# Seven block products for every two-sign unit, in one step of a five-step pipeline

## The chip, the cores and the metric

The kernel runs on one core of a Trainium2 chip. It uses TensorE (PE, matrix products), VectorE (DVE), ScalarE (ACT), GpSimd (POOL) and the DMA queues, of which SyncE (SP) and GpSimd issue the transfers. The metric is the time of one execution on the device in microseconds; before the change it is 1177.75 us, the median of three runs (1176.4 to 1179.02).

## The reference

The input x has 8 batches of 3136 tokens with 256 features. A two-dimensional Fourier transform over tokens and features is taken and its real part kept; each of the 25088 tokens then goes through a layer with 1024 hidden features:

```python
X = np.fft.fft(np.fft.fft(x, axis=1), axis=2).real
h = X.reshape(25088, 256) @ w_in                  # 256 -> 1024
e = np.exp(h - h.max(-1)); sm = e / (e.sum(-1) + 1e-09)
solu = h * sm
ln = (solu - solu.mean(-1)) / np.sqrt(solu.var(-1) + 1e-06) * g_ln
out = ln @ w_out                                  # 1024 -> 256
```

All of it is computed in fp32.

## The kernel before, in words

The transform over 3136 tokens is split as 49 x 64. The batches go in four pairs (`Pair`). For a pair, chunks of x are loaded twice, straight (`xa`, SP queue) and mirrored (`xb`, an indirect load on GpSimd's queue). `add_mirror` sums the two (GpSimd, L137 and L138; VectorE for the first pair), `fold` sums and subtracts mirrored features (VectorE, L128 and L129), `transform1` does the length-49 transform on TensorE (L182) and `keep` writes it to DRAM, from where `turn` reads it back in another order. There are 8 chunks of two parts each.

A *unit* is one frequency k1 of one pair: 128 tokens with the sign + and, except where k1 is 0, 128 more with the sign -. There are 25 units a pair, 100 in all; 96 have two signs and 4 (0, 25, 50, 75) have one. One pass of the main loop is a *step*; in step i the newest unit is i. For a unit:

- `transform2` (TensorE, L210) and the ScalarE copy `take2` (L216) give q; `spread` moves one row of it to a column r by a small DMA.
- `up` (TensorE, L238, 8 instructions of 512 columns) gives the even and the odd half of h in two PSUM tiles; `even` (VectorE, L244) and `join` for each sign (VectorE, L252) make h and its maximum.
- `expo` (ScalarE, L259 and L261) negates the maximum and takes u = exp(h - max) with its sum; `product` (VectorE, L268) makes u = h * u with its sum; `square` (ScalarE, L275) sums squares.
- `turn_blocks` (VectorE, L304) transposes blocks of 32 x 32 and `move_blocks` (16 DMAs on the SP queue for two units, L330) puts the blocks in their places, so that uT holds u transposed.
- `stats` (ScalarE) and `power` (GpSimd, L291) give the factor rs of each token.
- The *down* product u @ w_out is done lag = 4 steps later. `down` does it plainly: 8 blocks of 128 x 256 for a sign (L443). For odd two-sign units (`by_seven`) the two signs are done together: with u of both signs as a 2 x 2 matrix of blocks A11, A12 (sign +) and A21, A22 (sign -), a scheme of seven block products p1 to p7 (L359, each 4 blocks of 128 x 128) takes the place of eight. It needs four sums of blocks, S0 to S3, which GpSimd makes in `sums` (L354); p5 reads S0, p6 S1, p3 S3 and p7 S2. Weight sums Ws are made once. ScalarE's `keep` (L390) and VectorE's `finish` (L394) put the output together, `store` writes it: the + sign by SP, the - sign by an indirect DMA of GpSimd (L454).

The whole program is a hand schedule: each engine takes its instructions in the order in which the code emits them, and waits on semaphores for its inputs and for the buffers that it overwrites. In step i the seven products of an odd unit are spread over two steps: p1, p4, p2 in one, p5, p6, p3, p7 in the next, whose unit is done plainly beside them. `sums` and `power` come at the beginning of a step, and a step's order is, in short, `even`, `up`, `join`, first products, `expo`, other products, `product`, `square`, `turn_blocks`, `move_blocks`. Work for the next pair of batches (`ahead`) comes at the end: the mirror sum of a chunk in step f, its fold in f + 1, both parts of its first transform in f + 3, with f = 3, 5, ... 17 for pair 1, 27 to 41 for pair 2 and 51 to 65 for pair 3. S is one buffer (pool of one), uT, v, h and u are doubled.

Of the kernel before, what the change touches and what calls it, by code (L numbers as in the profile page):

```python
# [35 lines left out]
def kernel(  # L36
# [57 lines left out]

    def result(i):

        return ps_m.tile([P, 2 * D], FP32, tag=f"m{i % 4}", name="ps_m")
# [28 lines left out]
    def fold_features(o, i, copy):  # L126
        up, down = i[:, :, 1:128], i[:, :, 255:128:-1]
        nc.vector.tensor_tensor(out=o[:, :, 1:128], in0=up, in1=down, op=ALU.add)  # L128
        nc.vector.tensor_tensor(out=o[:, :, 129:256], in0=up, in1=down, op=ALU.subtract)  # L129
        copy(o[:, :, 0:129:128], i[:, :, 0:129:128])  # L130

    def add_mirror(pr, c, engine):

        xa, xb, _ = pr.raw[c]
        n = CH - 1 if c == NC - 1 else CH
        a, rb = xa[:, 0:n, :], xb[:, ::-1, :][:, 0:n, :]
        engine.tensor_tensor(out=a[:, :, 1:D], in0=a[:, :, 1:D], in1=rb[:, :, D - 1 : 0 : -1], op=ALU.add)  # L137
        engine.tensor_tensor(out=a[:, :, 0:1], in0=a[:, :, 0:1], in1=rb[:, :, 0:1], op=ALU.add)  # L138

    def fold(pr, c):  # L140

        xa, _, x0 = pr.raw.pop(c)
        y = xpool.tile([PR, CH, D], FP32, tag="y", name="y")
        copy = nc.scalar.copy if pr.p else nc.vector.tensor_copy
        fold_features(y, xa, copy)
        pr.y[c] = y
        if c == NC - 1:
            pr.y0 = xpool.tile([PR, 1, D], FP32, tag="y0", name="y0", bufs=1)
            fold_features(pr.y0, x0, copy)

    def transform1(pr, s):
# [6 lines left out]
        if l == 0:  # L158
# [3 lines left out]
            elif c < 4:  # L162
                z = fpool.tile([P, FF], FP32, tag="u", name="z_u", bufs=2)
                pr.z = z[0:ZR].rearrange("p (l d) -> p l d", l=CH)
# [82 lines left out]
    def join(t, s):  # L247

        if s == 0:
# [3 lines left out]
                                       scalar=-3.0e38, op0=ALU.add, op1=ALU.max, accum_out=t.nmax[:, s : s + 1])  # L253

    def expo(t, s):
        if s == 0:
            t.esum = small.tile([P, 2], FP32, tag="esum", name="esum")
            t.neg = small.tile([P, 2], FP32, tag="neg", name="neg")
        nc.scalar.mul(out=t.neg[:, s : s + 1], in_=t.nmax[:, s : s + 1], mul=-1.0)  # L259
        t.u[s] = fpool.tile([P, FF], FP32, tag="u", name="u", bufs=2)  # L260
        nc.scalar.activation(out=t.u[s], in_=t.h[s], func=ACT.Exp, bias=t.neg[:, s : s + 1],  # L261
                             accum_out=t.esum[:, s : s + 1])

    def product(t, s):
# [3 lines left out]
        nc.vector.scalar_tensor_tensor(out=t.u[s], in0=t.h[s], scalar=1.0, in1=t.u[s], op0=ALU.mult,  # L268
# [24 lines left out]
    class Batch:  # L293


        def __init__(self, by_blocks):
            if by_blocks:
                self.v = fpool.tile([P, 2, FF, 2], FP32, tag="v", name="v32", bufs=2)
            self.uT = fpool.tile([P, 2, KF, 4, 64], FP32, tag="uT", name="uT", bufs=2)

    def turn_blocks(t, s):

        for o in (s,) if len(t.signs) == 2 else (0, 1):
            nc.vector.transpose(out=t.batch.v[:, t.w, :, o], in_=t.u[s])  # L304
# [43 lines left out]
    def sums(t):  # L348

        A11, A12, A21, A22 = blocks(t)  # L350
        t.S = spool.tile([P, 4, KF // 2, P], FP32, tag="S", name="S")
        for j, (a, b, op) in enumerate(((A21, A22, ALU.add), (t.S[:, 0], A11, ALU.subtract),
                                        (A11, A21, ALU.subtract), (A12, t.S[:, 1], ALU.subtract))):
            nc.gpsimd.tensor_tensor(out=t.S[:, j], in0=a, in1=b, op=op)  # L354
# [5 lines left out]

    banks = []

    def bank(i):

        if not banks:
            banks.extend(result(j) for j in (2, 3, 1))
        return banks[i]

    class Down:
# [4 lines left out]

        def __init__(self, t, fresh):
            self.t = t
            self.C11, self.X, self.P53 = (bank(i)[:, 0:P] for i in range(3))
            self.A11, self.A12, _, self.A22 = blocks(t)
            for s in range(2):
                t.ot[s] = fpool.tile([P, D], FP32, tag="ot", name="ot", bufs=10)  # L380
# [3 lines left out]

        def place(self, s, half):
            return self.t.ot[s][:, half * P : (half + 1) * P]

        def keep(self, s, half, ps):

            nc.scalar.mul(out=self.place(s, half), in_=ps, mul=self.t.rs[:, s : s + 1])  # L390

        def add(self, s, half, ps):
            o = self.place(s, half)
            nc.vector.scalar_tensor_tensor(out=o, in0=ps, scalar=self.t.rs[:, s : s + 1], in1=o, op0=ALU.mult, op1=ALU.add)  # L394
# [7 lines left out]
        def p4(self):  # L402
            product7(self.P53, self.A22, Ws[:, 3], True)

        def keep4(self):
            self.keep(1, 0, self.P53)
# [4 lines left out]
        def keep11(self):  # L411
            self.keep(0, 0, self.C11)

        def p5(self):
            product7(self.P53, self.t.S[:, 0], Ws[:, 0], True)

        def keep5(self):
            self.keep(1, 1, self.P53)

        def p6(self):  # L420
            product7(self.X, self.t.S[:, 1], Ws[:, 1])

        def keep6(self):
            self.keep(0, 1, self.X)

        def p3(self):
            product7(self.P53, self.t.S[:, 3], Wo[:, KF // 2 :, P:])

        def p7(self):
            product7(self.X, self.t.S[:, 2], Ws[:, 2])  # L430

        def finish(self):
            self.add(0, 1, self.P53)
            self.add(1, 1, self.X)
            self.add(1, 0, self.X)
# [529 lines left out]
```

## Time and profile before

| what | value |
|---|---|
| median of 3 runs | 1177.75 us (1176.4 to 1179.02) |
| span of the profiled execution, which the page gives as its time | 1174.4 us |
| TensorE busy | 1132.6 us, 96% |
| VectorE busy | 1005.7 us, 86% |
| ScalarE busy | 762.4 us, 65% |
| GpSimd busy | 598.2 us, 51% |
| DMA, hardware queue and software queue | 60.4% and 12.4% of 16 engines |
| mean granted TensorE clock | 0.998 |
| first `up` of unit 5 and of unit 99 | 97.1 and 1127.0 us |

The page comes from one execution. A busy share is the part of the span in which an engine had an instruction running; matmuls overlap their neighbours, so a group's mean time is longer than the pitch at which they follow each other. The column "idle before" of a group says how long the engine had stood idle ahead of the group's instructions and who ended most of that. The timeline lists instructions of one kind in a row as one entry.

### The profile page before, as it was taken

The numbers are of one execution on the slowest core, as the hardware profiler recorded it, in microseconds if no ns is written. First come the engines' busy times: TensorE is split into PE (matmuls) and PEld (weight loads), VectorE is DVE, ScalarE is ACT, GpSimd is POOL, SyncE is SP. The second block draws the span as 40 slices with busy tenths as digits, with TensorE's granted clock in tenths as the row PEclk, the third lists the DMA queues.
The fourth block names the chain that finished last, engine by engine and source line by source line (L and its number), as shares of the span: only waits on it lengthen the run. The fifth ranks groups of instructions, "written<-read, shape, count | busy, mean of one in ns | idle before, by whom it ended". The sixth has DMA issues, their size and how long they took to land. (4 is left out here: it accounts for less than half of the span.)

```text
span 1174.4 us, 18577 instructions
## 1 busy us (share of the span) xinstructions
PE 1132.6 (96%) x5850; PEld 881.2 (75%) x5850; DVE 1005.7 (86%) x1376; ACT 762.4 (65%) x1841; POOL 598.2 (51%) x558
## 2 busy tenths in 40 slices
PE   2988999999999999999999999999999999999997
PEld 1556787777877787877877777778777787778787
DVE  7789999998878999998879999999887898888870
ACT  4577666757756766767656666676666676677651
POOL 3036666563465566563556666554544334433444
PEclk9999999999999999999999999999999999999999
DMA  9672998865988998865879898865775565745553
GB/s 243 196 186 71 180 183 180 176 141 127 180 185 167 182 167 186 176 141 135 176 146 188 176 188 183 172 146 133 153 154 135 135 152 125 154 108 137 130 116 109
DMA packets 458465, 185.55 MB, mean 158 GB/s; under 512 B 425750, under 2 KB 440350, under 8 KB 458368
## 3 DMA queue, kind: packets, MB, share of 16 engines
q1 hardware_dynamic: 444608, 146.22, 60.4%
q0 software_dynamic: 13760, 38.16, 12.4%
q8 instruction: 47, 0.77, 0.3%
q14 instruction: 50, 0.41, 0.1%
HBM read 44.78 MB, written 38.80 MB: 71 GB/s over the span
## 5 line engine op out<-in xcount | busy, mean ns | idle before, releaser
L443 PE MATMUL ps_m<-Wo,uT 128*128 128x256 f32 x1632 | 369.2, 380 | 3.1 <-ACT uT L321 2.1
L238 PE MATMUL ps_h<-Wi,q 128*128 128x512 f32 x800 | 360.8, 593 | 3.0 <-DVE nmax L252 2.1
L443 PEld LDWEIGHTS ps_m<-Wo,uT 128*128 128x128 f32 x1632 | 314.2, 196 | 33.8 <-ACT uT L321 2.4
L268 DVE SCALAR_TENSOR_TENSOR u<-h,u 128x1024 f32<-128x1024 f32 x196 | 266.1, 1366 | 50.5 <-ACT u L261 36.1
L238 PEld LDWEIGHTS ps_h<-Wi,q 128*128 128x128 f32 x800 | 145.9, 190 | 149.9 <-issue 140.0
L275 ACT ACTIVATE h<-u,usum 128x1024 f32<-128x1024 f32 x196 | 224.4, 1145 | 34.3 <-DVE u L268 33.0
L354 POOL TENSOR_TENSOR S<-uT 128x512 f32<-128x512 f32 x94 | 130.4, 1387 | 208.5 <-issue 138.7
L261 ACT ACTIVATE u<-h,neg 128x1024 f32<-128x1024 f32 x196 | 225.3, 1150 | 6.4
L304 DVE STREAM_TRANSPOSE v<-u 128x1024 f32<-128x1024 f32 x192 | 227.8, 1226 | 0.1
L291 POOL TENSOR_TENSOR rs<-v,neg_half 128x2 f32<-128x2 f32 (+1 forms) x100 | 71.7, 717 | 251.8 <-ACT v L284 251.7
L252 DVE CUSTOM_DVE_ANT_0 h<-ev,ps_h 128x1024 f32<-128x1024 f32 x100 | 122.2, 1222 | 33.3 <-PE ps_h L238 23.5
L244 DVE SCALAR_TENSOR_TENSOR ev<-w_mid,r,ps_h 128x1024 f32<-128x1024 f32 x100 | 126.7, 1267 | 25.6 <-PE ps_h L238 20.6
L359 PE MATMUL ps_m<-Ws,S 128*128 128x128 f32 x1128 | 141.5, 275 | 1.8 <-ACT ot L390 1.8
L216 ACT COPY q<-ps_m 128x256 f32<-128x256 f32 x100 | 36.8, 368 | 159.4 <-PE ps_m L210 155.9
L359 PEld LDWEIGHTS ps_m<-Ws,S 128*128 128x128 f32 x1128 | 133.6, 192 | 2.7 <-issue 1.6
L252 DVE CUSTOM_DVE_ANT_0 h<-h,ps_h 128x1024 f32<-128x1024 f32 x96 | 117.3, 1221 | 13.8
L454 POOL DMA_INDIRECT out_dram<-ot,idx x96 | 100.8, 1050 | 30.7 <-issue 18.7
L359 PE MATMUL ps_m<-Wo,uT 128*128 128x128 f32 x752 | 104.2, 282 | 0.1
L182 PE MATMUL ps_m<-y,F 98*100 98x258 f32 (+3 forms) x288 | 73.4, 390 | 24.7 <-DVE y L130 21.8
L210 PEld LDWEIGHTS ps_m<-T,g 128*128 128x128 f32 x400 | 60.2, 191 | 49.1 <-issue 41.7
L359 PEld LDWEIGHTS ps_m<-Wo,uT 128*128 128x128 f32 x752 | 96.1, 196 | 0.9 <-issue 0.5
L259 ACT ACTIVATE neg<-nmax 128x1 f32<-128x1 f32 x196 | 38.4, 196 | 81.5 <-DVE nmax L252 73.6
(87 smaller groups left out, 1186.7 us busy)
## 6 DMA issues: line engine op xcount, KB each, us to landing
uT<-v SPq DMA_DIRECT2D x752, 128.0 KB
out_dram<-ot SPq DMA_DIRECT2D x100, 128.0 KB
g<-zd POOLq DMA_DIRECT2D x72, 160.0 KB, 5.6
xa<-in_x_dram SPq DMA_DIRECT2D x28, 392.0 KB
zd<-z SPq DMA_DIRECT2D x24, 400.0 KB
raw_in<-in_moe_w_in_dram SPq DMA_DIRECT2D x4, 512.0 KB
raw_out<-in_moe_w_out_dram SPq DMA_DIRECT2D x2, 1024.0 KB
r<-q SPq DMA_DIRECT2D x100, 0.5 KB
```

The costliest lines, as they stand in the source:

```text
L182: nc.tensor.matmul(o[..., cs], F[:, 2 * t + h, :], i[..., cs], start=first, stop=True, skip_group_check=True)
L238: nc.tensor.matmul(ps[:, fs], t.q[:, c * P : (c + 1) * P], Wi[:, c, fs], start=True, stop=True)
L244: nc.vector.scalar_tensor_tensor(out=t.ev, in0=w_mid, scalar=t.r, in1=ps, op0=ALU.mult, op1=ALU.add)
L252: nc.vector.tensor_tensor_reduce(out=t.h[s], in0=t.h[0] if s else t.ev, in1=t.odd, scale=1.0 if s else -0.5, scalar=-3.0e38, op0=ALU.add, ...
L261: nc.scalar.activation(out=t.u[s], in_=t.h[s], func=ACT.Exp, bias=t.neg[:, s : s + 1], accum_out=t.esum[:, s : s + 1])
L268: nc.vector.scalar_tensor_tensor(out=t.u[s], in0=t.h[s], scalar=1.0, in1=t.u[s], op0=ALU.mult, op1=ALU.mult, accum_out=t.usum[:, s : s + 1])
L275: nc.scalar.activation(out=t.h[s], in_=t.u[s], func=ACT.Square, bias=t.usum[:, s : s + 1], scale=-float(FF), accum_out=t.ssq[:, s : s + 1])
L304: nc.vector.transpose(out=t.batch.v[:, t.w, :, o], in_=t.u[s])
L354: nc.gpsimd.tensor_tensor(out=t.S[:, j], in0=a, in1=b, op=op)
L359: nc.tensor.matmul(o, a[:, c], b[:, c], start=start and c == 0, stop=c == n - 1, skip_group_check=True)
L443: nc.tensor.matmul(ps, uT[:, c, :, s], Wo[:, c, :], start=(c == 0), stop=(c == KF - 1))
L454: dma = nc.gpsimd.indirect_dma_start(out=out, out_offset=bass.IndirectOffsetOnAxis(ap=idx[:, i : i + 1], axis=0), in_=t.ot[s], in_offset=None)
```

## The change

What the new code does, part by part:

- `by_seven` holds for every two-sign unit but the last (95 units, where it was 47). All seven products are done in one step, five steps behind the unit (lag 5), in the order p1, p4, p5, first-transform part, p2, p6, p3, p7. Plain products are left for the one-sign units and the last unit.
- C11 and X share one PSUM tile of two banks, p4's and p5's results share a bank. ScalarE evicts each pair in one instruction (`keep_p`, `keep_cx`); `finish` has two VectorE instructions, of 128 and 256 columns. `keep_cx` stands ahead of the step's `expo` on ScalarE, `finish` between the two `product`s on VectorE.
- S is four tiles, still one of each. `sums` for the next unit is emitted after p7, and its first sum gets a wait on the last `product` of the unit before (`behind`). So does each mirror sum.
- The mirror sum, the fold and the first transform of a chunk are cut in halves, one to a step: mirror in f and f + 1, fold in f + 1 and f + 2 (now between `join` and `product`), transform in f + 3 and f + 4. The sum of feature 0 goes from GpSimd to VectorE (one small instruction a half). The loads of x are emitted a step later.
- `move_blocks` is emitted in the next even step, after `sums`, where it was emitted at the end of the odd step.
- u is one tile for both signs, and one transpose instruction turns both (`turn_both`).
- h is kept negated (the weights' scale changes its sign), so `join` takes a minimum, the exponential uses scale -1 and the negation of the maximum is gone.

```diff
-    def sums(t):
+    S = [spool.tile([P, KF // 2, P], FP32, tag=f"S{j}", name=f"S{j}") for j in range(4)]
+
+    def sums(t, prv):
         A11, A12, A21, A22 = blocks(t)
...
+        for j, a, b, op in ((0, A21, A22, ALU.add), (1, S[0], A11, ALU.subtract), (3, A12, S[1], ALU.subtract),
+                            (2, A11, A21, ALU.subtract)):
+            i = nc.gpsimd.tensor_tensor(out=S[j], in0=a, in1=b, op=op)
+            if j == 0 and prv:
+                behind(i, prv)
...
+            self.CX = pair_cx[:, :, 0:P]
+            self.C11, self.X = (self.CX[:, i] for i in range(2))
+            self.PP = result(1)[:, 0 : 2 * P]
+            self.P4, self.P5 = (self.PP[:, i * P : (i + 1) * P] for i in range(2))
...
         def finish(self):
-            self.add(0, 1, self.P53)
-            self.add(1, 1, self.X)
-            self.add(1, 0, self.X)
+            o = self.t.ot[0][:, P:]
+            nc.vector.scalar_tensor_tensor(out=o, in0=self.P5, scalar=self.t.rs[:, 0:1], in1=o, op0=ALU.mult, op1=ALU.add)
+            o = self.t.ot[1].rearrange("p (i d) -> p i d", i=2)
+            nc.vector.scalar_tensor_tensor(out=o, in0=self.X.unsqueeze(1).to_broadcast([P, 2, P]),
+                                           scalar=self.t.rs[:, 1:2], in1=o, op0=ALU.mult, op1=ALU.add)
...
+            if work == "mirror" and a in (0, 1):
+                behind(add_mirror(pr, c, nc.gpsimd, a), units[i - 1])
+            if work == "fold" and a in (1, 2):
+                fold_part(pr, c, a - 1)
+
+    def behind(i, t):
+
+        tc.add_manual_dep(i.ins, t.last.ins.name,
+                          mybir.DependencyInfo(mybir.DependencyClass.Sync, mybir.DependencyReason.DATA),
+                          reason="two operands at a time from SBUF")
...
-        lag = 4
+        lag = 5
...
-            return i % 2 and i < len(units) - 1 and len(units[i].signs) == 2
+            return 0 <= i < len(units) - 1 and len(units[i].signs) == 2
...
                 enter(i)
                 even(cur, up(cur, 0))
                 cur.odd = up(cur, 1)
                 second_transform(i + 2)
+            if seven:
+                new = Down(old, fresh)
+                fresh = False
+                new.p1()
+                new.seed()
+            if prv:
+                stats(prv)
+            if seven:
+                new.p4()
+                new.p5()
+                new.keep_p()
+            elif old:
+                plain = [(s, down(old, s, result(s + 1)[:, 0:D])) for s in old.signs]
+            if cur:
+                other_pairs(i, ahead_pe)
+            if seven:
+                new.p2()
+                new.p6()
+                new.keep_cx()
...
                 for s in cur.signs:
                     join(cur, s)
             if seven:
-                new = Down(old, i == whole + 1)
-                new.p1()
-                new.seed()
...
+                new.p3()
+                new.p7()
+            if cur:
+                other_pairs(i, ahead, "mirror")
+            if by_seven(i + 1 - lag):
+                sums(units[i + 1 - lag], prv)
+            if i % 2 == 0 and whole < i - 1 < len(units) - 2:
+                batches[i // 2 - 1].place()
+                move_blocks(batches[i // 2 - 1], slice(0, 2))
+            if prv:
+                power(prv)
+            if kept and 1 in kept.signs:
+                store(kept, 1)
+            if cur:
+                other_pairs(i, ahead, "fold")
+                for s in cur.signs:
+                    expo(cur, s)
+                product(cur, 0)
+            if seven:
+                new.finish()
...
+                if 1 in cur.signs:
+                    product(cur, 1)
                 for s in cur.signs:
-                    product(cur, s)
-                square(cur, 0)
...
+                    square(cur, s)
+                turn_both(cur)
```

## The prediction

> **What bounds the kernel now.** I read the page's busy shares first, then its groups of instructions, then the timeline of a few steps, then the list of waits. A step is one pass of the main loop, one unit.
>
> The page's shares and four groups (line, engine, operation, tiles, count | busy us, mean ns | idle before):
>
> ```profile
> PE 1132.6 (96%) x5850; PEld 881.2 (75%) x5850; DVE 1005.7 (86%) x1376; ACT 762.4 (65%) x1841; POOL 598.2 (51%) x558
> ...
> L443 PE MATMUL ps_m<-Wo,uT 128*128 128x256 f32 x1632 | 369.2, 380 | 3.1 <-ACT uT L321 2.1
> L238 PE MATMUL ps_h<-Wi,q 128*128 128x512 f32 x800 | 360.8, 593 | 3.0 <-DVE nmax L252 2.1
> ...
> L268 DVE SCALAR_TENSOR_TENSOR u<-h,u 128x1024 f32<-128x1024 f32 x196 | 266.1, 1366 | 50.5 <-ACT u L261 36.1
> ...
> L354 POOL TENSOR_TENSOR S<-uT 128x512 f32<-128x512 f32 x94 | 130.4, 1387 | 208.5 <-issue 138.7
> ```
>
> TensorE has almost no idle time. Each fp32 matmul is two instructions (102 plain products x 8 blocks x 2 = 1632). VectorE stands at 86%, which leaves room on average only.
>
> The timeline (start us, duration, engine, line, operation) gives the true pitch of a matmul, because a group's mean overlaps its neighbour:
>
> ```profile
> 602.12 1.95 PE L359 MATMUL ps_m<-Ws,S 128*128 128x128 f32 x16
> ...
> 609.15 3.60 PE L238 MATMUL ps_h<-Wi,q 128*128 128x512 f32 x8
> ...
> 613.03 1.11 PE L359 MATMUL ps_m<-Wo,uT 128*128 128x128 f32 x8
> 613.97 3.63 PE L443 MATMUL ps_m<-Wo,uT 128*128 128x256 f32 x16
> ```
>
> (duration - one mean)/(count - 1): 0.112 us for 128 columns from S, 0.118 from uT, 0.216 for 256 columns, 0.43 for 512. Starts of the first L238 matmul at 609.15, 619.31, 630.22: a seven-step takes 10.16, a plain one 10.91, mean 10.535. These are exactly the sums of the pitches: TensorE does not wait. With two parts of the first transform in a pair of steps the pair takes 22.80 (12.64 + 10.16), mean 11.40.
>
> The second thing to see is how VectorE and GpSimd meet (same view):
>
> ```profile
> 630.48 1.51 POOL L354 TENSOR_TENSOR S<-uT 128x512 f32<-128x512 f32 x1
> 631.11 1.42 DVE L128 TENSOR_TENSOR y<-xa 98x508 f32<-98x508 f32 x1
> 632.07 1.61 POOL L354 TENSOR_TENSOR S<-S,uT 128x512 f32<-128x512 f32 x1
> 632.46 1.76 DVE L129 TENSOR_TENSOR y<-xa 98x508 f32<-98x508 f32 x1
> ...
> 638.38 2.37 POOL L137 TENSOR_TENSOR xa<-xa,xb 98x1020 f32<-98x1020 f32 x1
> 639.14 2.71 DVE L268 SCALAR_TENSOR_TENSOR u<-h,u 128x1024 f32<-128x1024 f32 x1 [0.17 <-ACT u L261]
> 640.71 1.20 POOL L138 TENSOR_TENSOR xa<-xa,xb 98x4 f32<-98x4 f32 x1
> 641.77 1.21 DVE L268 SCALAR_TENSOR_TENSOR u<-h,u 128x1024 f32<-128x1024 f32 x1
> ```
>
> The product issued at 639.14 ends at 641.85, 1.14 after the mirror sum lets go at 640.71: it stood still meanwhile (clear: 1.23). The tiny GpSimd sum after it then waits for the product. The folds (clear 0.68) and the sums S alternate in the same way, one for one. Joins (1.22), L244 (1.27) and transposes (1.2) show no stretching.
>
> **What the Trainium skill says.** "SBUF — State Buffer", section "Who interferes with whom": a VectorE instruction with two SBUF inputs contends with a GpSimd instruction that reads SBUF, and whoever issues first has the shared port for its whole instruction. The lines above agree (640.71). "TensorE: Matmul & The Clock Gate", section "Back-to-back issue gap": spacing is set by the weight load and the matmul together; here 128 columns still cost about half of 256 (0.112-0.118 against 0.216), so seven products do save. "GPSIMD Engine Reference", section 3.1: about 2.6 cycles an element for a two-input fp32 sum, at 1.2 GHz 1.1 us for 512 elements (estimate); measured clear 1.04 to 1.50, which I use.
>
> **The change, part by part.**
>
> TensorE: a unit's plain products are 32 x 0.216 = 6.91; seven are 24 x 0.118 + 32 x 0.112 = 6.42. 48 more units: -24 us if TensorE stays the bound. An ordinary step is then 8 x 0.43 + 4 x 0.112 + 6.42 = 10.30, one with a part of the first transform 11.16 (+4 x 0.216).
>
> GpSimd: 48 x 4 more sums at 1.50, 1.25, 1.25, 1.04 (start to start) = 5.04 a unit, +242 us; 1.2 for a mirror half, 0.72 power, 1.05 store: 9 of 11 us, it fits. But S is still one buffer of each. S0 can be written only after p5 has read the old S0, S1 after p6, S3 after p3, S2 after p7. p5 ends 6.7 us into a step; the previous product ends about 5. So the added wait costs nothing in ordinary steps (behind it: sums, power, store, loads), and S1, S3, S2 run from p6's end (8.5, with the transform 9.37) for 3.54 us. That is where VectorE comes to its fold and products.
>
> VectorE: L244 1.44, join 1.37, join 1.40, product 1.25, finish 0.74 (0.35 + 0.39, from L394's 0.25 per 128 columns), product 1.15, transposes 2.29 = 9.6 in each step, from starts between 634.93 and 645.21. A fold half is 2 x 0.35 plus a small add, 0.8.
>
> Ordinary step: the product is ready at about 10.7, waits for S3 (ends 11.2), runs to 12.35; S2 runs behind it to 13.4 while VectorE finishes from PSUM; the second product waits 0.2. 7.6 us of VectorE work later the next one is ready at 21.0 = 10.7 of the next step. This closes at 10.30: gain 0.235 x 42 steps = -9.9.
>
> Fold and transform steps (6-19, 30-43, 54-67, 42 of them): three VectorE operations with two SBUF inputs stand before the product and alternate with S3 and S2, so the product comes only after S2. Now there is a loop: p1 waits for the previous finish (one PSUM tile holds C11 and X, and p1's first matmul in the built order has a wait on VectorE); p1, p4, p5, transform, p2, p6 5.49; 0.2 to GpSimd; S1, S3, S2 3.54; fold 0.8; product 1.25; finish 0.74; 0.1 back. Sum 12.1. The other way round, second product, square (1.23), q copy (0.37), whose bank the transform needs, comes to the same. 12.1 - 11.40 = 0.7 a step, +29; some 3 off for entries into the three stretches, where slack is used up first: +26.
>
> Fold-only steps (5, 28, 29, 52, 53): the loop without transform is 11.2, +0.67 each, +3. Transform-only (20, 21, 44, 45, 68, 69): no fold, 11.16, -1.4.
>
> Block moves: an even step's 16 issues (15.5 us of SP queue at 599.81) now wait for p2 at 7.6 and land near 25; the sums start at 20.6 + 6.7 = 27.3 and their first use is 8 us later. Hidden; if not, each us late beyond that is 1 us per two steps. Stores and r queue behind them on SP and are needed a step later. The loads of x go out one step later, two steps (23 us) ahead of their sum; an xb load lands in 6.9: hidden. Pair 1's first transform ends in step 21, not 20, in the step of its turn; its writes stand behind step 20's block moves, and unit 25 needs the turned tile in step 23: +2 (0 to 5). Tail: 8 move issues of 0.6 on GpSimd stand ahead of the last sums, and the last sign's indirect store comes last: +3 (0 to 6). Negation: 196 x 0.196 off ScalarE, 65% busy, worth nothing in time. Merged evictions and transposes: same work, nothing.
>
> Unknown: the doubled transpose and the minimum in the join have no row; taken as two old transposes and as the maximum. 0.3 us either way in an ordinary step stays inside VectorE's slack (10.30 against 9.6 plus 0.7 of locks, which is the whole of it), so a slower form costs up to 12.
>
> Sum: +26 - 9.9 + 3 - 1.4 + 2 + 3 = +23 on the span 1174.4, 1197. The median of the runs lies 3.35 above the span; that is kept: **1200**.
>
> **Rivals.** (1) TensorE stays the bound throughout, faster. For: before, the same collisions (1.4-1.8 us a fold) cost no TensorE idle time. Against: there nothing of TensorE waited for the finish in the same step. It decides if the loop falls by 1 us to 11.16, that is if S2 gets done before the fold comes. -24 + 5: 1158. (2) Ordinary steps are caught too: S2 before the product makes their loop 10.7; 42 x 0.4 = +17: 1217. (3) The locks cost half, 11.5 a fold step: +4 - 10 + 7: 1179. (4) The block moves arrive late: 1 us per two steps, +40: above 1220. That the named wait does not what it says (sums held by S, not by the product) is in my forecast.
>
> **How the numbers follow.** Forecast 0.62 (own range 1190 to 1212), rival 1 0.20, 2 0.08, 3 0.07, 4 0.03. 1160 to 1217 leaves out rival 4 and about half of rival 1. About 0.2% can be told from no change. Faster: rival 1 and a part of 3, 0.22; within 0.2%: 0.04; slower: 0.74.
>
> **What would show it.** Starts of the first up matmul: 12 us apart in steps 6-19, 10.3 in 80-98. Waits of p1 on the finish's ps_cx, or of the first transform on the q copy, summing to 30 us or so; y's two folds at 1 us and more each; GpSimd's S waiting for PE in every step, not for VectorE. Wrong if TensorE's busy share stays at 96% and fold steps keep 11.2, or if S0 waits for the transfers.

## The result, and the profile after

The changed kernel takes 1221.78 us (median of 4 runs, 1218.24 to 1223.54) where the kernel before takes 1177.61 (4 runs): ratio 1.0363, 95% interval 1.0339 to 1.0386, slower by 44 us. The forecast was 1200 with a range of 1160 to 1217; the direction was right, the time lies 4.8 us above the range. The spans of the two profiled executions are 1174.4 and 1221.6 us, so 47.2 us have to be found. (The forecast's step from span to median, 3.35 us, is only 0.2 here, so in spans the miss is 24.5 us and in medians 21.8.)

The page of the changed kernel: the line of busy shares, then groups (line, engine, operation, tiles, count | busy us, mean ns | idle before, and who ended most of it).

```profile
PE 1129.8 (92%) x7002; PEld 897.1 (73%) x7002; DVE 1103.2 (90%) x1428; ACT 741.1 (61%) x1626; POOL 935.1 (77%) x750
...
L391 POOL TENSOR_TENSOR S<-uT 128x512 f32<-128x512 f32 x190 | 296.0, 1558 | 56.3 <-PE ps_m L398 51.8
L294 DVE SCALAR_TENSOR_TENSOR u<-h,u 128x1024 f32<-128x1024 f32 x196 | 286.4, 1464 | 18.1 <-ACT u L287 17.9
...
L398 PE MATMUL ps_cx<-Wo,uT 128*128 128x128 f32 x1520 | 216.1, 286 | 34.4 <-DVE ot L453 33.8
```

TensorE's share falls from 96% to 92%: it now waits. Its busy time is about what it was (1129.8 us against 1132.6), although the forecast took 24 us of work away. The work did go: in e7 below the same 7002 matmuls are busy for 1109.5 us, 23 us less than before. The changed kernel stands 20 us above that, a part of which is a slower clock (0.987 of the full one granted in the mean, 0.998 before and in e7; see the last section). VectorE gained 98 us of busy time, GpSimd 337. The product's mean rose from 1366 to 1464 ns; the timeline below shows it standing while a sum S runs. The last group is p1 and p2 together. It has a new idle time of 34 us before it, ended by VectorE's `finish` (L453); that is p1's.

The list of waits of the changed kernel (who waits <- whom, total us, times, longest):

```profile
ACT h L301 <- DVE u L294: 220.1, 186, 4.5
...
POOL S L391 <- PE ps_cx L398: 56.5, 61, 1.7
POOL S L391 <- PE ps_m L398: 51.8, 45, 3.3
...
PE ps_cx L398 <- DVE ot L453: 33.8, 45, 3.2
...
POOL xa L135 <- DVE u L294: 19.9, 16, 4.2
```

The sums S wait for TensorE, which still reads the old S; they are not among the work that waits for VectorE's product, although the wait was added to them. Only the mirror sums (L135) show that wait, 16 times. TensorE's largest wait of the main loop is the fourth line.

A step's length is the distance between the first `up` matmuls (L238 before, L265 after) of two units. Added up over the kinds of steps, this is where the 47.2 us are; the stall of a step's late `finish` falls into the next interval, because the fold of step i runs while `up` of step i + 1 has already begun.

| stretch (first `up` to first `up`) | before, us | after, us | difference | predicted |
|---|---|---|---|---|
| start of the span to unit 5 | 97.1 | 104.5 | +7.4 | 0 |
| 42 fold and transform steps | 478.9 | 503.3 | +24.3 | +26 |
| 5 fold-only steps (5, 28, 29, 52, 53) | 50.4 | 62.4 | +12.0 | +3 |
| 6 transform-only steps | 70.4 | 71.8 | +1.4 | -1.4 |
| 41 ordinary steps | 430.1 | 419.3 | -10.8 | -9.9 |
| unit 25's turn (step 23, counted in the row above) | 10.16 | 10.28 | +0.1 | +2 |
| from unit 99 to the end | 47.4 | 60.3 | +12.9 | +3 |

One border needs a word. Unit 0's plain down product moved from step 4 to step 5, because the lag is 5: step 4 fell from 13.07 to 9.69 us and step 5 rose from 6.93 to 10.49. So 3.6 of the 12.0 us of the fold-only steps belong to the start, which up to unit 6 lost 10.9 us (115.0 against 104.1). The other 8.4 us are those of steps 52 and 53 (+8.6), with 28 and 29 a little shorter.

The timeline of the changed kernel (start us, duration, engine, line, operation, idle before) in two steps, 15 to 16 with fold and transform, and then an ordinary one:

```profile
235.94 1.29 POOL L391 TENSOR_TENSOR S<-uT,S 128x512 f32<-128x512 f32 x1
...
235.96 1.55 DVE L142 TENSOR_TENSOR y<-xa 98x254 f32<-98x254 f32 x1
...
237.19 1.22 POOL L391 TENSOR_TENSOR S<-uT 128x512 f32<-128x512 f32 x1
237.43 1.25 DVE L143 TENSOR_TENSOR y<-xa 98x254 f32<-98x254 f32 x1
...
238.68 1.21 DVE L294 SCALAR_TENSOR_TENSOR u<-h,u 128x1024 f32<-128x1024 f32 x1
...
240.09 0.47 DVE L453 SCALAR_TENSOR_TENSOR ot<-ps_cx,rs,ot 128x256 f32<-128x256 f32 x1
...
240.61 1.21 PE L398 MATMUL ps_cx<-Wo,uT 128*128 128x128 f32 x8 [0.53 <-DVE ot L453]
...
245.29 1.06 PE L398 MATMUL ps_cx<-Ws,S 128*128 128x128 f32 x8
...
246.50 1.30 POOL L391 TENSOR_TENSOR S<-S,uT 128x512 f32<-128x512 f32 x1 [1.16 <-PE ps_cx L398]
...
906.41 1.28 POOL L391 TENSOR_TENSOR S<-S,uT 128x512 f32<-128x512 f32 x1
...
906.80 1.98 DVE L294 SCALAR_TENSOR_TENSOR u<-h,u 128x1024 f32<-128x1024 f32 x1
907.78 2.16 POOL L391 TENSOR_TENSOR S<-uT,S 128x512 f32<-128x512 f32 x1
...
910.33 1.11 PE L398 MATMUL ps_cx<-Wo,uT 128*128 128x128 f32 x8
```

In the first step the two large instructions of the fold half (0.41 us each where no sum runs, see e1) take 1.55 and 1.25 us: each stands until a sum, S3 and then S2, has let go of the port. Then come product and `finish`, and p1, which writes the tile that `finish` reads, starts 0.53 us late at 240.61. The next S1 starts at 246.50, behind p6, which begins at 245.29. Such steps are 11.94 us apart. In the ordinary step the product itself takes a turn with the sums (1.98 instead of 1.21 us, then S3 2.16 instead of 1.29), but there is room: p1 follows `transform2` at once, and the step is 10.28 us, near the 10.30 of the summed matmul pitches.

### The profile page after: what moved, and what is told of

It is laid out like the page before. It is cut to its first block, busy times and chain, and to the rows that moved or that the text cites. A ratio compares the mean times of both kernels' runs of the same rounds, so it can differ in the third digit from the quotient of the medians.

```text
span 1221.6 us, 21291 instructions
## 1 busy us (share of the span) xinstructions
PE 1129.8 (92%) x7002; PEld 897.1 (73%) x7002; DVE 1103.2 (90%) x1428; ACT 741.1 (61%) x1626; POOL 935.1 (77%) x750
## 3 DMA queue, kind: packets, MB, share of 16 engines
q0 software_dynamic: 13760, 38.16, 11.9%
## 5 line engine op out<-in xcount | busy, mean ns | idle before, releaser
L265 PE MATMUL ps_h<-Wi,q 128*128 128x512 f32 x800 | 365.1, 599 | 3.9 <-DVE nmax L279 2.6
L391 POOL TENSOR_TENSOR S<-uT 128x512 f32<-128x512 f32 x190 | 296.0, 1558 | 56.3 <-PE ps_m L398 51.8
L294 DVE SCALAR_TENSOR_TENSOR u<-h,u 128x1024 f32<-128x1024 f32 x196 | 286.4, 1464 | 18.1 <-ACT u L287 17.9
L265 PEld LDWEIGHTS ps_h<-Wi,q 128*128 128x128 f32 x800 | 146.1, 193 | 151.8 <-issue 144.3
L398 PE MATMUL ps_cx<-Wo,uT 128*128 128x128 f32 x1520 | 216.1, 286 | 34.4 <-DVE ot L453 33.8
L287 ACT ACTIVATE u<-h,nmax 128x1024 f32<-128x1024 f32 x196 | 224.8, 1147 | 21.6 <-DVE nmax L279 9.6
L398 PEld LDWEIGHTS ps_cx<-Wo,uT 128*128 128x128 f32 x1520 | 198.9, 198 | 47.3 <-DVE ot L453 43.2
L337 DVE STREAM_TRANSPOSE v<-u 128x2048 f32<-128x2048 f32 x93 | 215.3, 2315 | 3.2
L398 PE MATMUL ps_cx<-Ws,S 128*128 128x128 f32 x1520 | 200.8, 275 | 0.0
L398 PEld LDWEIGHTS ps_cx<-Ws,S 128*128 128x128 f32 x1520 | 184.4, 191 | 0.0
L391 POOL TENSOR_TENSOR S<-S,uT 128x512 f32<-128x512 f32 x95 | 125.2, 1318 | 59.3 <-PE ps_cx L398 56.5
L391 POOL TENSOR_TENSOR S<-uT,S 128x512 f32<-128x512 f32 x95 | 137.3, 1445 | 7.4
L398 PE MATMUL ps_m<-Ws,uT 128*128 128x128 f32 x760 | 105.8, 283 | 0.0
```

Source lines behind the costliest of these rows:

```text
L265: nc.tensor.matmul(ps[:, fs], t.q[:, c * P : (c + 1) * P], Wi[:, c, fs], start=True, stop=True)
L294: t.last = nc.vector.scalar_tensor_tensor(out=t.u[s], in0=t.h[s], scalar=-1.0, in1=t.u[s], op0=ALU.mult, op1=ALU.mult, accum_out=t.usum[:, ...
L337: nc.vector.transpose(out=t.batch.v[:, t.w].rearrange("p f o -> p o f"), in_=t.both)
L391: i = nc.gpsimd.tensor_tensor(out=S[j], in0=a, in1=b, op=op)
L398: nc.tensor.matmul(o, a[:, c], b[:, c], start=start and c == 0, stop=c == n - 1, skip_group_check=True)
```

## The experiments

All times are against runs of the kernel before on the same chip (median 1178.35 us for the first four, 1177.91 for the next four, 1177.80 for the last three). The standing theory, A, was the table above: separate losses, each with its own cause. The rivals are named with each run. Gains and losses are differences of medians; where a stretch is given, it comes from the profiled execution.

### e1: the fold half behind the products

```diff
-                other_pairs(i, ahead, "fold")
                 for s in cur.signs:
                     expo(cur, s)
                 product(cur, 0)
...
                     square(cur, s)
+                other_pairs(i, ahead, "fold")
                 turn_both(cur)
```

GpSimd's wait is put on the fold's last instruction, which is now VectorE's last one with two SBUF inputs.

> The fold's half is moved from ahead of the first product to behind the second one, and the wait of GpSimd's next mirror half or sum is put on the fold's last instruction. Theory A (loop in fold steps: p1 to p6, S1, S3, S2, fold, product, finish, p1; its length 11.94 us): without fold and S2 in the loop, steps 6 to 19, 31 to 43 and 56 to 67 fall from 11.94 to TensorE's own 11.16, the wait of p1 on finish goes from 33.8 us to under 8, and the time falls by 30 to 35 us, to about 1188. Theory B (VectorE is simply overfull in these steps): its work is the same, steps stay at 11.6 or more and the time above 1208.

Measured: 1194.95 us, ratio 1.0159 (1.0131 to 1.0187): 26.8 us of the 44 are gone, a little less than theory A's 30 to 35. The fold and transform steps fall from 503.3 to 481.3 us. 26 of the 42 are at 11.14 us, TensorE's own work; the other 16, most of them at the beginning of a stretch and behind a turn, hold 13.4 us more, and there A had promised too much. p1's wait for `finish` fell from 33.8 to 6.3 us, and theory B is out: VectorE has the same work, and the time is well under B's 1208. Timeline of e1 in such a step (12):

```profile
180.99 1.29 POOL L392 TENSOR_TENSOR S<-uT,S 128x512 f32<-128x512 f32 x1
...
181.41 1.96 DVE L295 SCALAR_TENSOR_TENSOR u<-h,u 128x1024 f32<-128x1024 f32 x1
...
183.95 1.40 DVE L295 SCALAR_TENSOR_TENSOR u<-h,u 128x1024 f32<-128x1024 f32 x1
...
184.31 1.10 PE L399 MATMUL ps_cx<-Wo,uT 128*128 128x128 f32 x8
...
185.28 0.41 DVE L142 TENSOR_TENSOR y<-xa 98x254 f32<-98x254 f32 x1
185.61 0.41 DVE L143 TENSOR_TENSOR y<-xa 98x254 f32<-98x254 f32 x1
```

The product now meets the sum, and stretches to 1.96 us, yet p1 doesn't wait; the folds come when GpSimd has nothing but `power` to do and take 0.41 us each. So what makes the loop in these steps is the fold's place ahead of the product, not the number of sums. The tail stayed at 60.3 us and steps 52 to 54 at 43.6 (47.0 in the changed kernel), so these have other causes.

### e3: both added waits left out

```diff
-                behind(add_mirror(pr, c, nc.gpsimd, a), units[i - 1])
+                add_mirror(pr, c, nc.gpsimd, a)
...
-            if j == 0 and prv:
-                behind(i, prv)
```

> The two added waits of GpSimd on VectorE's product are left out, nothing else. Theory A (S held by the products that read the old S): sums start where they did, and the port is taken in turn either way; within 4 us of 1222, most likely within 2. Theory B (the wait protects the product): products stretch by 1 us or more in fold steps, 1240 or more. Theory C (the wait itself delays the sums): 20 us faster or more.

Measured: 1241.61 us, ratio 1.0548 (1.0524 to 1.0572), 20 us slower than with the waits: theory B, and not the A that I held. Many fold and transform steps now take about 13.4 us, the others about 11.9, and they add up to 523.9. Timeline of e3:

```profile
177.73 2.76 DVE L294 SCALAR_TENSOR_TENSOR u<-h,u 128x1024 f32<-128x1024 f32 x1
...
178.11 1.28 POOL L135 TENSOR_TENSOR xa<-xa,xb 98x510 f32<-98x510 f32 x1
...
182.08 1.11 PE L209 MATMUL ps_m<-y,F 98*100 98x258 f32 x4 [1.17 <-ACT q L243]
```

The mirror half starts under the late second product, which ends 1.1 us after the mirror half lets go. Square and the q copy come after it on ScalarE, and the first transform, which needs q's bank, waits 1.17 us. So the two waits together are worth 20 us with this order. That it is the mirror sum's is read from the traces (in the changed kernel the sums S don't show that wait); no run leaves out one of the two alone. What I had expected was wrong, for I had looked at the sums alone. One thing stays open: by the recorded starts the product was first here, by 0.38 us, as in ten such places of this trace, and yet it was the one that stood. GpSimd's recorded spans are rough, so who really came first can't be told.

### e2: the first loads of pair 3 ahead of the block moves

```diff
             if cur:
+                other_pairs(i, ahead, "first")
                 enter(i)
```

The first two chunks of pair 3 are loaded at the beginning of step 50, not at its end, and those of pair 2 at the beginning of step 25, where no block moves are; the condition on these loads moves with the call.

> The first two chunks of the last pair are loaded at the beginning of step 50, ahead of step 50's block moves on the SP queue, and not at its end. If the 12.3 us wait of GpSimd's mirror sum for xa, with the sums S of the seven products queued behind it, is what stretches steps 52 to 54 (46.97 us where 34.2 is usual), they fall to 34 to 36 us and the time falls by 11 to 13 us, to about 1209. If another transfer or the lower granted clock is the cause, they stay over 40 us.

Timeline of the changed kernel in steps 51 to 54, which this run is about:

```profile
629.28 16.08 SPq L366 DMA_DIRECT2D uT<-v  x16
...
645.41 1.04 SPq L118 DMA_DIRECT2D xa<-in_x_dram  x2
...
651.70 1.27 POOL L135 TENSOR_TENSOR xa<-xa,xb 98x510 f32<-98x510 f32 x1 [12.28 <-DMA xa<-in_x_dram]
...
654.46 2.08 PE L398 MATMUL ps_m<-Ws,S 128*128 128x128 f32 x8 [6.53 <-POOL S L391]
...
670.28 2.41 POOL L225 DMA_DIRECT2D g<-zd  x4
...
678.92 2.08 PE L398 MATMUL ps_cx<-Wo,uT 128*128 128x128 f32 x8 [3.23 <-DVE ot L453]
...
680.79 1.91 PE L398 MATMUL ps_m<-Ws,uT 128*128 128x128 f32 x8
```

The load of xa stands behind step 50's 16 block moves on SP's queue (16.08 us) and is issued at 645.41, though the code emits it in step 50, whose first `up` is at 621.4; GpSimd's first mirror half needs it, stands 12.28 us, and behind it stand the sums, for which p5 waits 6.53 us. Step 52 takes 18.46 us. In e2 step 52 is 10.28 us and the three steps 37.3 us in place of 47.0; the time is 1212.96, ratio 1.0304 (1.0275 to 1.0333), 9 us less, where a fall of 11 to 13 us, and 34 to 36 us for the three steps, had been expected. What stays is step 54 at 15.35: the four issues of `turn` (L225, 2.4 us of GpSimd) stand ahead of the mirror half and the sums. They don't make the stall alone: in e6, which leaves them there but has the fold behind the products, step 54 takes 11.14, and 55 and 56 only 2.5 us more than in e2.

### e4: C11 and X in two tiles

```diff
-    pair_cx = ps_m.tile([P, 2, 2 * D], FP32, tag="cx", name="ps_cx")
+    m_tiles = [ps_m.tile([P, 2 * D], FP32, tag=f"m{i}", name=f"ps_m{i}") for i in range(4)]
...
-            nc.scalar.mul(out=self.t.ot[0].rearrange("p (i d) -> p i d", i=2), in_=self.CX, mul=self.t.rs[:, 0:1])
+            for i, ps in enumerate((self.C11, self.X)):
+                nc.scalar.mul(out=self.t.ot[0][:, i * P : (i + 1) * P], in_=ps, mul=self.t.rs[:, 0:1])
```

> C11 and X lie in two PSUM tiles, as before the change, and are evicted by two ScalarE instructions. p1 then need not wait for finish. If that wait alone closes the loop, fold steps fall to about 11.2 and the time by 35 us or more. If the other way round (second product, square, q copy, first transform) is as long, as the prediction had it, they fall by only 0.1 to 0.3 a step. Besides, the first transform of pair 0 no longer waits for each eviction of a shared tile: the first up starts at 57 rather than 62.5. Together about 1205 to 1212.

Measured: 1210.48 us, ratio 1.0283 (1.0252 to 1.0314). p1 no longer waits for `finish`, but the fold and transform steps fall by 0.13 us only, to 11.81. The waits of e4:

```profile
PE ps_m L208 <- ACT q L242: 21.4, 40, 1.4
```

The first transform waits in 40 steps for the q copy behind the second product: the prediction's other way round, of almost the same length. In the profiled execution these 42 steps give 5.4 us of what is gained, and the start as much: from the first `up` of unit 0 to that of unit 6 it takes 46.9 us, not 52.5 (47.9 before the change). The reason is to be seen in the changed kernel's timeline, at `turn_whole`'s transposes into the shared tile:

```profile
83.67 0.82 PE L352 MATMUL ps_cx<-ident,u 128*128 128x128 f32 x4 [2.44 <-ACT uT L357]
...
85.14 4.74 PE L265 MATMUL ps_h<-Wi,q 128*128 128x512 f32 x8
```

Two results share one tile and so one wait; the second of them waits for the eviction of the first. The same happens in the next two steps (2.42 and 2.43 us), and each time the `up` that follows is slow, here 4.74 us in place of 3.60: the clock granted from 84.0 us on for 3.4 us is half. In e4 the clock is full all through these steps. That the first `up` of unit 0 came at 57.4, as expected, says nothing about the split: in e3, which has the shared tile, it came at 57.4 too.

### e5: the stores one step after the products

```diff
-        for i in range(whole + 1, len(units) + lag + 3):
+        for i in range(whole + 1, len(units) + lag + 1):
...
-            kept = units[i - lag - 3] if i >= lag + 3 else None
+            kept = units[i - lag - 1] if i >= lag + 1 else None
```

> Only edit: a unit's two stores go out one step after its down products instead of three. Theory A (the tail's end is GpSimd's chain of indirect stores, about 3.2 us apart, which starts late because each store is held back three steps): the stretch from the last matmul to the end falls from 12.2 us to about 6 to 8, the time to 1214 to 1217 us. Theory B (the tail is set by TensorE's own part, 48.1 us against 40.7 before, and the stores only follow): the time moves by less than 2 us, 1220 to 1223 us. In the loop neither theory expects a change: fold steps with a transform stay at 11.9 us, ordinary ones at 10.28.

Timeline of the changed kernel's end:

```profile
1174.10 1.21 PE L398 MATMUL ps_cx<-Wo,uT 128*128 128x128 f32 x8 [2.83 <-DVE ot L453]
...
1181.34 1.21 PE L398 MATMUL ps_cx<-Wo,uT 128*128 128x128 f32 x8 [0.57 <-DVE ot L453]
...
1191.17 4.72 POOL L366 DMA_DIRECT2D uT<-v  x8
...
1195.89 1.55 POOL L391 TENSOR_TENSOR S<-uT 128x512 f32<-128x512 f32 x1
...
1201.33 1.05 POOL L473 DMA_INDIRECT out_dram<-ot,idx  x1 [0.16 <-issue]
...
1204.79 0.98 POOL L473 DMA_INDIRECT out_dram<-ot,idx  x1 [2.41 <-DMA out_dram<-ot,idx]
...
1217.67 0.96 POOL L473 DMA_INDIRECT out_dram<-ot,idx  x1 [2.19 <-issue]
```

Six indirect stores come at the end, one every 3.2 us, each after the one before has landed; the first of them stands behind eight block-move issues and the last sums. In e5 four are left at that point and the first of them goes out at 1196.22: the stretch from the last matmul to the end is 5.7 us in place of 12.2, the time 1213.31 us, ratio 1.0296 (1.0262 to 1.0331), 8.5 us less. Theory A is borne out, with the stretch and the time just under its figures (6 to 8 us, 1214 to 1217). The tail gives 6.5 us; the other 2 lie before unit 99, where the edit was not expected to act, and are not explained.

### e6 and e8: the cures together, and without the split tile

e6 is e1, e2, e4 and e5 in one; e8 the same without e4.

> Four edits together: fold halves behind the second product (e1), pair 3's first two chunks loaded ahead of step 50's block moves (e2), C11 and X in two PSUM tiles (e4), stores one step after the products (e5). Theory A (the 47 us of the changed kernel's span are four separate losses, in the fold steps, in steps 52 to 54, at the start and in the tail, so that their cures add): 1221.8 minus 26.8, 9 and 11 as measured alone and about 6 for the stores is about 1169 us, between 1163 and 1175: below the kernel before (1178). Rival B (the cures hide the same time, so that a cured wait is followed by the next one): at least 1180 us. Fold steps with a transform at 11.14 us, steps 52 to 54 together at most 38 us, first up of unit 5 at about 91 to 97 us, last matmul to end at most 9 us.

> e6 without e4: C11 and X share one PSUM tile as in the changed kernel. Theory A (the shared tile costs the start: turn_whole and the first transform wait for the eviction of the other half): the first up of unit 5 comes 5 to 8 us later than in e6, the loop's steps are the same to 0.1 us, the time is 5 to 10 us above e6. Rival B (the start's loss was warm-up and loads that vary from run to run, and the shared tile matters little): within 3 us of e6.

e6 takes 1172.39 us, ratio 0.9957 (0.994 to 0.9975): below the kernel before. With what each edit took off alone (26.8, 8.8, 11.3 and 8.5 us) it would be 1166, so they add, but for 6 us, within theory A's 1163 to 1175. Steps 52 to 54 are at 31.7 us. e8 takes 1177.57, ratio 1.0002 (0.9989 to 1.0015), 5.2 us above e6, as theory A had it at its lower end; its loop is as quick as e6's (1018.7 us from unit 5 to 99, against 1021.3), its start the slower one: 51.5 us from unit 0 to unit 6, against 47.7. The profiled execution of e8 was its slowest (1185.63 us), with 8 us more ahead of the first `up` than in e6, so the traces give the place of the loss better than its size.

### e7 and b1: who issues the turn

```diff
-            turn(pr, at.index(step))
+            turn(pr, at.index(step), nc.sync)
```

e7 is e6 with this edit, b1 the kernel before with it.

> e6 with one edit more: the four transfers of a later pair's turn are issued by SyncE, no longer by GpSimd ahead of the next step's mirror half and sums. Theory A (in steps 53, 54, 29 to 31 and 55 to 56 those issues, 2.4 us of GpSimd, delay S0 to S3, and p5 waits for them): 2 to 5 us below e6, step 54 at most 13 us. Rival B (the queue of SyncE is held by the turn's wait for zd's landing and by the block moves, so that the spread of r, loads and stores go late): equal to e6 or up to 10 us above it.

> The kernel before with e7's last edit alone: turn's transfers of the later pairs issued by SyncE. It tells whether e7's gain over e6 (8 us) belongs to the new schedule, whose GpSimd is fuller, or would have come to the kernel before too. Theory A (GpSimd of the kernel before has slack, 51% busy against 77% of the changed one, and its TensorE hardly waits): within 3 us of the kernel before. Rival B (steps 29, 31 and 54 of the kernel before are stretched by the same issues): 3 to 8 us faster.

e7 takes 1163.98 us, ratio 0.9878 (0.9853 to 0.9903): 8.4 us below e6, more than was expected. The gain is in the steps after each turn (30: 9.88 to 8.21, 39: 13.04 to 11.14, 64: 13.06 to 11.36, and others), in all 7.9 us of the fold and transform steps. Timeline of e6 in steps 37 to 39:

```profile
461.09 2.40 POOL L225 DMA_DIRECT2D g<-zd  x4
...
478.24 1.29 POOL L391 TENSOR_TENSOR S<-S,uT 128x512 f32<-128x512 f32 x1
478.37 2.24 DVE L294 SCALAR_TENSOR_TENSOR u<-h,u 128x1024 f32<-128x1024 f32 x1
...
484.55 1.11 PE L209 MATMUL ps_m<-y,F 98*100 98x258 f32 x4 [0.79 <-ACT q L243]
```

GpSimd has no slack for the 2.4 us of a turn in these steps: a step and a half later its sums are still late. S1 starts just ahead of the product, which stands 1.0 us for it (2.24 in place of 1.21); square and q copy come after that, and the first transform waits 0.79 us. In the kernel before the same edit costs 5.3 us (1183.13, ratio 1.0046, 1.0029 to 1.0063), which neither theory had. Timeline of b1:

```profile
291.76 12.97 SPq L330 DMA_DIRECT2D uT<-v  x16
...
304.91 2.38 SPq L198 DMA_DIRECT2D g<-zd  x4
...
310.81 1.19 PE L210 MATMUL ps_m<-T,g 128*128 128x128 f32 x4 [6.11 <-DMA g<-zd]
```

On SP's queue the turn of pair 1 is behind 16 block moves, and unit 25's second transform waits 6.1 us for it: step 23 takes 18.12 us. So e7's gain belongs to the new schedule. That its GpSimd is fuller (81% to 84% busy in e6 and e7, 51% before) and its block moves come later is the likely reason; b1 shows only that the old schedule does not have the gain.

### e9: e7 without the two waits

The diff is that of e3.

> e7 with both added waits left out: mirror halves and S0 no longer wait for VectorE's product. Theory A (without the wait the mirror half or S0 starts beside the second product, takes the port first and makes it 1.2 to 1.4 us longer, as in e3, where the second product took 2.76 us; behind it stand the square and the q copy, whose bank the first transform needs): fold steps with a transform lengthen from 11.14 to 11.7 or more, the time is 15 to 30 us above e7. Rival B (only the fold standing ahead of the first product made the missing wait dear in e3; with the fold behind the products there is room for it): within 4 us of e7.

Measured: 1171.14 us, ratio 0.9936 (0.9918 to 0.9955), 7 us above e7: between the two theories. The fold steps stay at 11.14 us, so with the fold behind the products the waits are worth nothing there, as rival B said. Steps 6, 55 and 56 are longer by 1.8, 4.2 and 1.4 us, others are shorter or longer by less, together 5 us in the loop, and the start differs by 3; why the entries into a stretch are the ones that suffer was not followed up.

### e10: the last block moves on ScalarE

```diff
-                move_blocks(batches[-1], slice(w, w + 1), (nc.sync, nc.gpsimd) if w else (nc.sync,))
+                move_blocks(batches[-1], slice(w, w + 1), (nc.sync, nc.scalar) if w else (nc.sync,))
```

> e7 with half of the last unit's block moves issued by ScalarE in place of GpSimd (8 issues of 0.6 us there stand ahead of the last four sums, and p5 waited 1.99 us for S0 at 1140.83 of e7). Theory A (those issues are what is late in the tail): the last sums come about 3 to 4 us earlier, TensorE's wait is gone, the time falls by 2 to 3.5 us. Rival B (the end is set by the indirect stores, 3.2 us apart, whatever TensorE does, or ScalarE's evictions now stand behind the issues): within 1 us of e7, or above it.

Measured: 1161.05 us, ratio 0.9851 (0.9831 to 0.987), 2.9 us below e7 and the lowest median, though the two intervals overlap. Timeline of e10:

```profile
1130.97 6.28 ACTq L366 DMA_DIRECT2D uT<-v  x8
...
1137.65 1.21 PE L398 MATMUL ps_m<-Wo,uT 128*128 128x128 f32 x8 [2.45 <-ACT ps_m L422]
```

Its tail is 53.9 us against 56.7. But TensorE's part of the tail is no shorter (48.3 us against 48.1): p5's wait for S0 is gone and p2 waits 2.45 us instead for a ScalarE copy behind the eight issues. It is the stretch after the last matmul that fell, from 8.6 to 5.6 us. The sums do not come 3 to 4 us earlier, as A had it: counted from unit 99's first `up`, S0 starts 34.0 us on, against 34.6 in e7, because it now waits 4.1 us for the moved blocks to land, and the first of the last four stores goes out at 39.4 us, against 40.0. Then the four follow each other faster (from first to last 9.8 us, against 11.3); why was not followed up. So the time is as theory A said, but not by A's way.

## Why the prediction was right, and where it was wrong

The steady steps of the loop came out as forecast. What failed is three terms of the sum: the tail (+3 given, +12.9 measured), the loads of x that were called hidden (steps 52 to 54: about +2 given, +13.1 measured), and the start, which was put at nothing (+7.4 to unit 5, +10.9 to unit 6).

**The loop of the fold and transform steps: right.** 12.1 us was forecast, 11.94 measured, +26 against +24.3 in sum. The chain is the one that was drawn (folds between the sums S3 and S2, product, `finish`, p1), and e1, which takes the fold out of it, brings most of these steps to 11.14. The sum is better than its terms, and in that lucky. From p1's start at 240.61 to the next S1 at 246.50 it takes 5.89 us (5.69 forecast), and from the S1 before (234.56) to S2's end (238.41) 3.85 (3.54 forecast). Then the fold adds only 0.27 us (the product starts at 238.68; 0.8 forecast), because its first instruction has run between S3 and S2. e4 showed that the second way, over the q copy, is 11.81 us: cutting one leaves the other, as the prediction said. "SBUF — State Buffer", section "Who interferes with whom", on which this rested (whoever issues first has the shared port for its whole instruction), agrees here: an instruction of 0.41 us takes 1.55 beside a sum of 1.29 that was first. In e3 the recorded starts don't fit it, as was said there.

**The ordinary steps: right.** 10.30 forecast, 10.28 measured. The collision came one sum earlier than was drawn (the product stands for S1, and S3 for the product), but the slack took it. That seven products are shorter than eight held, and the unknown forms were harmless: the doubled transpose took 2.31 us, two old ones took 2.29 by the prediction's count, and the join with a minimum 1.22 as before. Rivals 1 to 3 are out for the changed kernel (11.94 us a fold step and 10.28 an ordinary one); rival 1's picture, TensorE as the bound at 11.14 us a fold step, is what e1 and e7 then reached.

**The tail: mis-sized.** +3 was given, +12.9 measured. 2.8 us of it are work and 4.6 idle time of TensorE (p1 behind `finish`, 2.83 once and 0.57 or 0.58 in each of the next three steps, with no `up` to cover it), and 5.5 come after the last matmul, in the chain of indirect stores. The prediction counted the eight issues on GpSimd and one last store, but behind them six stores follow at 3.2 us each; e5, which leaves four, makes the tail 6.5 us shorter.

**The loads of x: "hidden" was wrong at one place.** The prediction took them as two steps ahead of their sum. That holds for the later chunks; the first two of pair 3 are emitted at the end of step 50, one step ahead of their first mirror sum, and issued behind step 50's block moves on the same queue. Steps 52 to 54 took 13.1 us more than before, where the prediction's terms for them (0.67, 0.67 and 0.7) make 2. About 4 of the 13.1 us (an estimate from the starts of the matmul groups at 654.46 to 685.35, against their pace elsewhere) are not waiting but half clock after it. e2 gives back 9.7 of that, and e6, with the fold behind the products as well, all of it (31.7). The step that failed is the one that looked at a transfer's landing and not at the queue in front of it.

**The start: forgotten.** 0 was given, +7.4 measured to unit 5 and +10.9 to unit 6. The prediction spoke of the shared tile only in the loop. It also serves `turn_whole`; there the transposes wait 2.4 us a unit, and half clock follows. Of the 10.9 us 4.6 lie behind the first `up` of unit 0, and e4, which splits the tile, takes 5.5 off this stretch; between e6 and e8 the tile makes 3.8. The other 6.4 us lie before that `up`, which comes at 62.5 us; in e3, with the same code there, it comes at 57.4, and in e8 at 66.4. So this part varies from run to run, and how much of it is the change's stays open.

**Small terms.** Transform-only steps were put at 11.16 and took 12.0 in the mean: the stall of the last fold falls into steps 20, 44 and 68 (12.34), and 21, 45 and 69 take 11.60 us. Unit 25's turn cost nothing (+2 forecast): GpSimd's queue, unlike SP's in b1, passes the block moves. Rival 4, block moves that come late, was not seen: S0 waits for TensorE, not for the transfers. That the added waits do nothing was half right: the sums don't show them, but e3 shows 20 us, by its trace for the mirror halves.

Sum of the loop: +19.7 forecast with unit 25's turn, +26.9 measured; start and tail +3 forecast, +20.3 measured. So of the 24.5 us beyond the forecast 17.3 are at the ends of the program and 7.2 in its loop, these more than accounted for by steps 52 to 54 (11.1 beyond the forecast); without either part the time would have lain inside the range.

## What to carry to other kernels

Where two engines take turns at a port instruction by instruction, put short two-input work behind the long instruction that others wait for: ahead of it, each short one cost about the length of the other engine's instruction here (1.55 and 1.25 us in place of 0.41). When a change fills a queue, go through every transfer that it issues and what stands in front of it, the first loads of a phase and the last stores above all: here these two cost 9 and 8.5 us. A change that loses can hold a gain: six small repairs turned +44 us into -17.

## What had not been expected of the hardware

After an idle time TensorE can run at half pace for a while: eight matmuls of 128 columns took 2.08 and 1.91 us (654.46, 678.92, 680.79 of the changed kernel, after idle times of 6.5 and 3.2 us) in place of 1.06 to 1.11, so that a wait can cost more than its length. The trace's granted clock is half there for 6.8 us each time, and in the start of the changed kernel three times for 3.4 us, each after an idle time of 2.4 us; the three `up`s there took 4.74, 5.02 and 5.29 us in place of 3.60. In the kernel before, the clock is full from the first `up` to unit 99, and so it is in e6, e7 and e10. "TensorE: Matmul & The Clock Gate", section "Part 1: The HAM clock gate", says that the clock is halved after an idle window of about 3.4 us; the prediction had not used it. The traces agree on the half clock and on the length of the windows, but not on the idle time that it takes: 2.42 us was enough in the start (93.62), while after 2.83 us in the tail (1174.10) and 2.45 us in e10 (1137.65) the matmuls ran at full pace.

GpSimd's indirect stores to one output don't overlap in these traces: they follow at 3.2 us although an issue takes 1.0, and each but the first waits 2.2 to 2.4 us, in four of the five cases by the trace for the landing of the one before. Whether the chip or only the program's own order asks for this was not tested.
